# Row sums of a softmax taken over partitions by GpSimd instead of TensorE

## The chip, the cores and the metric

The kernel runs on one core of one Trainium2 chip. The metric is the device time of one execution in microseconds (us), as the median of several runs. Five engines with queues of their own share the core: TensorE (PE in the profile, with weight loads listed as PEld), VectorE (DVE), ScalarE (ACT), GpSimd (POOL) and SyncE (SP), which here issues nearly all DMAs.

## The reference

Attention through 49 agent tokens, then a two-layer network with a PReLU between the layers. Two batches of 12480 tokens, 128 channels, hidden width 2048, all in float32.

```
scale = 1 / sqrt(128)
a2k     = softmax(scale * agents @ k^T)        # 49 x 12480 per batch
agent_v = a2k @ v                              # 49 x 128
q2a     = softmax(scale * q @ agents^T)        # 12480 x 49
x       = q2a @ agent_v                        # 24960 x 128 over both batches
h       = x @ w_in                             # 128 -> 2048
g       = max(h, 0) + alpha * min(h, 0)
out     = g @ w_out                            # 2048 -> 128
```

softmax(s) is e / (sum of e + 1e-9) with e = exp(s - max). What this case is about is the sum over the 49 agents in q2a, one number per token.

## The kernel before, in words

**The main loop.** Tokens stand in columns. A group is 480 tokens, 52 groups in all, and two groups make a pair k (0 to 25). The hidden layer is cut into 8 steps per group, so that a pair has 16 steps and the loop 416. In step s TensorE first runs `g1(s+2)`: it multiplies the unnormalised exponentials of a group, split into a high part `qmh` and a low part `qml`, by `agent_v @ w_in` (tile `sab`), 6 matmuls of 64 rows by 480 columns, into the PSUM tile `h`, of which there are two. ACT takes the positive part of `h` rounded (`rh`, line 974), DVE what the rounding left (`rl`, line 975). Then `g2(s)` multiplies `rh` and `rl` by the second layer's weights, 12 matmuls (line 990), into the accumulator `acc` of the group. After a group's eighth step three more matmuls (line 1001) add the linear part of the PReLU; ACT and DVE take the result out (lines 1006 and 1007), DVE turns it (`o_take`, line 1012), multiplies it by the reciprocal of the softmax's sum (`o_scale`, line 1017), and SP stores it (`o_store`, line 1035). The reciprocal is thus needed only at the very end of a group.

A matmul of 64 rows uses half of the array's rows. Two of them, one on rows 0 to 63 and one on rows 64 to 127, run side by side; a pair of them is called a slot below.

**The chain that makes the exponentials of pair k.** Its functions, in order, with the step at which each is issued, counted from the first step of pair k, s0 = 16k: `q_transpose` (-18), `q_hi` and `q_lo` (-16), `q_logits` (-14, 8 matmuls, line 864), `q_take` and `q_swap` (-13: an ACT copy and two DMAs on SP that swap halves of the partitions into tile `qw`), `q_add` (-11, line 890), `q_max` (-10, GpSimd's maximum over all 128 partitions, line 894), `q_sub` (-7, line 899), `q_exp_hi` (-6, line 903), `q_exp` and `q_split` (-5, lines 908 and 912), `q_sum` (4), `q_spread` (5) and `q_rec` (10). The list `CHAIN` holds these steps; `CHAIN_1` and `CHAIN_0` hold those of pairs 1 and 0. Since the chain of pair k+1 begins 18 steps before its own first step, it stands between the steps of pair k. A function given to `pre` is issued ahead of the step's g1, one given to `at` between g1 and g2. Every engine works through its own instructions in this written order; semaphores hold an instruction until what it reads is written and the buffer it writes is free.

The logits stand twice, on partitions 0 to 63 and 64 to 127, and `padb` sends the rows beyond 49 to zero through the exponential.

**The part that is changed.** `q_sum` multiplies `qmh` and `qml` by a matrix of ones: 4 matmuls (line 923) into the spare half of PSUM, which gives each token's sum on all partitions. `q_spread` copies these sums to the tile `sums` in SBUF by ACT (line 933) and has SP issue one DMA (line 939) that lays the sums of 960 tokens over the partitions. `q_rec` turns that on DVE, adds 1e-9 and takes the reciprocal (lines 946 to 951).

Tiles: `qs` and `qm` have one buffer each. `qs` holds the turned queries, then the logits, then (in place) the exponentials; `qm` holds the swapped half `qw` and then the maximum.

**Other work in the loop.** Steps 8 to 95 also make the logits of the second batch's keys (lines 538, 552, 572 to 574, 591), steps 96 to 187 its exponentials and products with v (lines 608 to 660), and around step 200 the weights `sab` of the second batch are made. GpSimd has little to do: the maxima, one per pair, and in steps 96 to 187 small memsets (line 612).

Of the kernel before, what the change touches and what calls it, by code (L numbers as in the profile page):

```python
# [9 lines left out]
F32 = mybir.dt.float32  # L10
F32R = mybir.dt.float32r
U32 = mybir.dt.uint32
AF = mybir.ActivationFunctionType
ALU = mybir.AluOpType
# [8 lines left out]
KEYS = (((1, 0), 6, 7), ((5, 3), 9, 14), ((9, 12), 14, 16))  # L23
VALUES = ((((0, 3, 1, 1), (3, 1, 4, 4)), 6), (((3, 0, 7, 8), (2, 8, 5, 6)), 10))
FOLD = (189, 195, 198, 202, 205, 206)
CHAIN = (-18, -16, -16, -14, -13, -13, -11, -10, -7, -6, -5, -5, 4, 5, 10)
CHAIN_0 = (-19, -18, -18, -11, -9, -6, 1, 6, 10, 15, 17, 19)
CHAIN_1 = (-14, -13, -13, -11, -10, -10, -10, -10, -8, -7, -5, -5, 4, 5, 10)
EARLY = (1, 3, 6, 6)
OUT = (4, 5, 5)  # L30

# [24 lines left out]
def kernel(  # L56
# [11 lines left out]
    nc = tc.nc  # L68
# [4 lines left out]
    P = 128  # L73
    HALF = 64
    NF = DFF // P
    GT = 480
    TB = GT // 32
# [13 lines left out]
    SCALE = 1.0 / math.sqrt(C)  # L91
# [5 lines left out]
    p1 = ctx.enter_context(tc.tile_pool(name="p1", bufs=1))  # L97
# [12 lines left out]
    def pair_tile(name, i=None):  # L110

        i = (step[0] // NM + 1) % 2 if i is None else i
        return late[i].tile([P, 2, 512], F32, tag="x", name=name)
# [21 lines left out]
    padb = const.tile([P, 1], F32, name="padb")  # L135
# [655 lines left out]
    gq = {}  # L791
# [20 lines left out]
    def flat(t):  # L812
        return t.rearrange("p h n -> p (h n)")
# [90 lines left out]
        gq["mh", k] = m  # L904

    def q_exp(k):
        e = gq["e", k] = gq.pop(("s", k))
        nc.scalar.activation(out=e, in_=e, func=AF.Exp, bias=padb, scale=SCALE)

    def q_split(k):  # L910
        m = p2.tile([P, 2, GT], F32R, tag="qml", name=f"qml{k}")
        nc.vector.tensor_tensor(out=m, in0=gq["e", k], in1=gq["mh", k], op=ALU.subtract)  # L912
        mh = gq.pop(("mh", k))
        gq.pop(("e", k))
        gq["mhl", k] = (m, mh)
        for i in range(2):
            gq["M", 2 * k + i] = (mh[:, i, :], m[:, i, :])

    def q_sum(k):
        t = gq["sum_ps", k] = pair_tile(f"qsum{k}")  # L920
        for n, x in enumerate(gq.pop(("mhl", k))):
            for i, (r0, r1) in enumerate(TILES):
                nc.tensor.matmul(  # L923
                    t[:, i, 0:GT], lhsT=ones[r0:r1, :], rhs=x[r0:r1, i, :],
                    start=n == 0, stop=n == 1,
                )

    def q_spread(k):
        if "sums" not in gq:
            t = gq["sums"] = p1m.tile([P, 1024], F32, tag="qsum", name="qsum")  # L930
            nc.gpsimd.memset(t[:, 2 * GT :], 1.0)
        t = gq["sums"]
        nc.scalar.copy(
            out=t[:, 0 : 2 * GT].rearrange("p (h n) -> p h n", h=2),
            in_=gq.pop(("sum_ps", k))[:, :, 0:GT],
        )

        x = p1m.tile([P, 32], F32, tag="qx", name=f"qx{k}")
        nc.sync.dma_start(
            out=x, in_=t.rearrange("(c o) (i j) -> c o i j", c=4, j=32)[:, 0, :, :]  # L940
        )
        gq["sum", k] = x

    def q_rec(k):
        t = p1m.tile([P, 32], F32, tag="qst", name=f"qst{k}")
        nc.vector.transpose(out=t, in_=gq.pop(("sum", k)))
        r = p2.tile([P, 2, TB, 1], F32, tag="qr", name=f"qr{k}")
        nc.vector.tensor_scalar(
            out=r.rearrange("p h t o -> p (h t o)"), in0=t[:, 0 : 2 * TB], scalar1=1e-9, scalar2=None, op0=ALU.add
        )  # L950
        nc.vector.reciprocal(out=r, in_=r)
        for i in range(2):
            gq["r", 2 * k + i] = r[:, i]
# [68 lines left out]
    def o_store(g):  # L1022
# [14 lines left out]
    q_chain = [  # L1037
        q_transpose, q_hi, q_lo, q_logits, q_take, q_swap, q_add, q_max,
        q_sub, q_exp_hi, q_exp, q_split, q_sum, q_spread, q_rec,
    ]  # L1040

# [5 lines left out]
    with tc.manual_schedule():  # L1047
# [46 lines left out]
        for n in range(7):  # L1094
            load, ops = (load_win, narrow_win) if n < 4 else (load_wo, narrow_wo)
            s = SLABS[n]
# [11 lines left out]
        def more():  # L1108
            f = next(loads, None)
            if f is not None:  # L1110
                f[1](*f[2:])
            return f

        while n_in < N_IN:
            f = more()
            n_in += f[1] not in (q_load_rows, load_alpha, load_late)
        for s in range(max(plan) + 1):
            for f, a in plan.pop(s, ()):
                f(*a)
                if f.__name__ == "total" or f in (k_turn, k_mix):  # L1120
                    while True:
                        f = more()
# [5 lines left out]
        p1m = ctx.enter_context(tc.tile_pool(name="p1m", bufs=1))  # L1128
# [22 lines left out]
        for i2 in range(NGT // 2):  # L1151
            s0 = 2 * NM * i2
            if i2 == 0:
                at(10, q_sum, 0)
                pre(11, q_spread, 0)
                at(13, q_rec, 0)
                continue
            steps = CHAIN if i2 > 1 else CHAIN_1
            if i2 > 1:
                at(max(0, s0 - LEADS[2]), q_load, i2)  # L1160
            for f, i in zip(q_chain, steps):
                (pre if f in (q_take, q_swap, q_spread) else at)(s0 + i, f, i2)
# [93 lines left out]
```

## Time and profile before

| what | value |
|---|---|
| median of 3 runs | 987.12 us (987.0 to 988.08) |
| span of the profiled execution, first to last instruction | 985.9 us |
| the profiled execution's own time | not listed apart from its span |
| median of the runs less the span | 1.2 us |
| busy PE / DVE / ACT / POOL | 971.7 / 837.7 / 626.4 / 89.8 us |
| granted TensorE clock over the span | 0.998 of full speed |

Busy time of PE counts every moment at which a matmul runs, be it on one half of the rows or on both. The durations of single matmuls overlap, since they are pipelined: what one costs is read from the distance between the starts of two, not from its length. PE's list in the timeline is in order of the start; "x2" joins neighbours of one kind.

### The profile page before, as it was taken

How to read it: one execution, taken by the hardware profiler on the slowest of the kernel's cores; microseconds unless marked ns; L12 is line 12 of the kernel's file. 1: busy time of each engine (PE TensorE's matmuls, PEld its weight loads, DVE VectorE, ACT ScalarE, POOL GpSimd, SP SyncE). 2: the span in 40 equal slices, each digit the busy share in tenths (PEclk: the TensorE clock that was granted, in tenths of full speed). 3: DMA queues.
4: the chain of work that ended last, by engine and by line, in shares of the span. 5: the costliest groups of instructions: out<-in, count | busy, mean ns of one | idle time of the engine just before them, and what ended most of it. 6: DMA issues, size and time to landing. Idle time of an engine off the chain costs nothing.

```text
span 985.9 us, 21716 instructions
## 1 busy us (share of the span) xinstructions
PE 971.7 (99%) x9046; PEld 927.0 (94%) x9046; DVE 837.7 (85%) x1054; ACT 626.4 (64%) x779; POOL 89.8 (9%) x67
## 2 busy tenths in 40 slices
PE   8989999999999999999999999999999999999997
PEld 5658999999989999999987999999999999999997
DVE  7887988998899999999987788788878887888775
ACT  5765655655667767777765666666666666666563
POOL 0011011011011011001101101100110111011100
PEclk9999999999999999999999999999999999999999
DMA  9933354444234234234312222212221223121201
GB/s 342 361 51 63 65 84 87 81 70 88 42 75 80 62 73 95 45 70 95 65 31 44 42 51 41 53 37 46 52 53 31 42 55 56 35 41 33 42 11 31
DMA packets 281027, 69.51 MB, mean 71 GB/s; under 512 B 259119, under 2 KB 273953, under 8 KB 280929
## 3 DMA queue, kind: packets, MB, share of 16 engines
q1 hardware_dynamic: 279937, 68.00, 33.0%
q8 instruction: 71, 1.16, 0.5%
q10 hardware_dynamic: 992, 0.12, 0.1%
q14 instruction: 27, 0.22, 0.1%
HBM read 42.59 MB, written 12.78 MB: 56 GB/s over the span
## 4 chain that ended last, share of the span: by engine, by line
PE 94%; DVE 2%; DMA 2%; ACT 1%; issue 0%; SPq 0%; ACTq 0%
PE acc L990 55%; PE h L968 27%; PE lg L864 2%; PE kl L552 2%; PE acc L1001 2%; PE av L650 1%; PE qsum L923 1%; DMA kw<-in_k_dram 1%; DMA win<-in_moe_w_in_dram 1%; PE a_ps L726 0%; DVE red L414 0%; PE avw L471 0%; PE ktp L388 0%; PE lin_ps L784 0%; PE etp L451 0%
## 5 line engine op out<-in xcount | busy, mean ns | idle before, releaser
L975 DVE SCALAR_TENSOR_TENSOR rl<-h,rh 128x960 fp32r<-128x960 f32 x416 | 478.2, 1150 | 123.1 <-ACT rh L974 120.8
L974 ACT ACTIVATE rh<-h 128x960 fp32r<-128x960 f32 x416 | 404.3, 972 | 270.1 <-PE h L968 262.1
L968 PE MATMUL h<-qmh,sab 64*128 64x480 f32 x1664 | 401.3, 378 | 0.7 <-DVE rl L975 0.5
L990 PE MATMUL acc<-rh,wl 64*128 64x480 f32 x1664 | 400.3, 378 | 0.0
L990 PE MATMUL acc<-rh,wh 64*128 64x480 f32 x1664 | 398.0, 375 | 0.0
L990 PE MATMUL acc<-rl,wh 64*128 64x480 f32 x1664 | 313.2, 377 | 0.0
L968 PEld LDWEIGHTS h<-qmh,sab 64*128 64x128 f32 x1664 | 247.2, 185 | 7.5 <-DVE rl L975 2.5
L990 PEld LDWEIGHTS acc<-rh,wl 64*128 64x128 f32 x1664 | 246.9, 184 | 5.9 <-issue 2.3
L990 PEld LDWEIGHTS acc<-rh,wh 64*128 64x128 f32 x1664 | 247.6, 184 | 2.9
L990 PEld LDWEIGHTS acc<-rl,wh 64*128 64x128 f32 x1664 | 223.6, 184 | 3.2
L968 PE MATMUL h<-qml,sab 64*128 64x480 f32 x832 | 222.7, 377 | 0.0
L894 POOL PARTITION_ALL_REDUCE qm<-qs x26 | 85.6, 3293 | 768.0 <-DVE qs L890 731.3
L968 PEld LDWEIGHTS h<-qml,sab 64*128 64x128 f32 x832 | 128.0, 185 | 1.7 <-DVE qml L912 0.2
L1006 ACT COPY os<-acc 128x480 f32<-128x480 f32 x52 | 29.2, 561 | 33.8 <-PE acc L1001 33.6
L1007 DVE TENSOR_TENSOR os<-acc,os 128x480 f32<-128x480 f32 x52 | 33.9, 651 | 2.7 <-ACT os L1006 2.4
L1012 DVE STREAM_TRANSPOSE ot<-os 128x480 f32<-128x480 f32 x52 | 34.7, 668 | 0.0
L903 ACT ACTIVATE qmh<-qs,padb 128x960 fp32r<-128x960 f32 x26 | 28.5, 1097 | 9.2 <-DVE qs L899 9.2
L1017 DVE TENSOR_TENSOR ot<-ot,qr 128x480 f32<-128x480 f32 x52 | 33.6, 645 | 0.1
L899 DVE TENSOR_TENSOR qs<-qs,qm 128x960 f32<-128x960 f32 x26 | 29.8, 1148 | 0.5 <-POOL qm L894 0.5
L890 DVE TENSOR_TENSOR qs<-qs,qw 128x960 f32<-128x960 f32 x25 | 28.7, 1148 | 1.7 <-DMA qw<-qs 1.7
L912 DVE TENSOR_TENSOR qml<-qs,qmh 128x960 fp32r<-128x960 f32 x26 | 29.8, 1148 | 0.0
L827 DVE STREAM_TRANSPOSE qt<-qin 128x960 f32<-128x960 f32 x25 | 29.2, 1167 | 0.0
(172 smaller groups left out, 802.8 us busy)
## 6 DMA issues: line engine op xcount, KB each, us to landing
out_dram<-ot SPq DMA_DIRECT2D x206, 60.0 KB
qin<-in_q_dram SPq DMA_DIRECT2D x200, 60.0 KB
qw<-qs SPq DMA_DIRECT2D x50, 240.0 KB
kw<-in_k_dram SPq DMA_DIRECT2D x12, 512.0 KB
vw<-in_v_dram SPq DMA_DIRECT2D x12, 512.0 KB
kb<-in_k_dram SPq DMA_DIRECT2D x96, 64.0 KB
v<-in_v_dram SPq DMA_DIRECT2D x24, 256.0 KB
win<-in_moe_w_in_dram SPq DMA_DIRECT2D x4, 512.0 KB
```

The costliest lines, as they stand in the source:

```text
L827: nc.vector.transpose(out=flat(t), in_=gq.pop(("in", k)).rearrange("p h t i -> p (h t i)"))
L894: nc.gpsimd.partition_all_reduce(flat(t), flat(gq["s", k]), P, ReduceOp.max)
L899: nc.vector.tensor_tensor(out=t, in0=t, in1=gq.pop(("m", k)), op=ALU.subtract)
L912: nc.vector.tensor_tensor(out=m, in0=gq["e", k], in1=gq["mh", k], op=ALU.subtract)
L968: nc.tensor.matmul(h[:, u, 0:GT], lhsT=w[a][r0:r1, f0 : f0 + P], rhs=x[r0:r1, :], start=n == 0, stop=n == 2,)
L974: nc.scalar.activation(out=rh, in_=h[:, :, 0:GT], func=AF.Relu)
L975: nc.vector.scalar_tensor_tensor(out=rl, in0=h[:, :, 0:GT], scalar=0.0, in1=rh, op0=ALU.max, op1=ALU.subtract)
L990: nc.tensor.matmul(acc[:, i, 0:GT], lhsT=a[r0:r1, 2 * m + u, :], rhs=x[r0:r1, u, :], start=m == 0 and n == 0, stop=False,)
L1006: nc.scalar.copy(out=t, in_=acc[:, 0, 0:GT])
L1007: nc.vector.tensor_tensor(out=t, in0=acc[:, 1, 0:GT], in1=t, op=ALU.add)
L1012: nc.vector.transpose(out=t.rearrange("p t i -> p (t i)"), in_=oo.pop(g))
L1017: nc.vector.tensor_tensor(out=t, in0=t, in1=gq.pop(("r", g)).to_broadcast([P, TB, 32]), op=ALU.mult)
```

## The change

The sums of pair 0 stay as they are. For every other pair `q_sum` issues two GpSimd instructions instead of four matmuls: a copy of one column of `qml` to a small tile (`gate`), which has to wait until the split has written it, and a sum over all 128 partitions of the exponentials straight into the tile `sums`. The ACT copy of `q_spread` falls away for these pairs. As the logits stand twice, the sum comes out doubled, and `q_rec` halves it in the instruction that adds 1e-9. The exponentials go to a new tile in the buffer of `qm`, not in place into `qs`. `q_sum` moves from step 4 to step -5, `q_spread` from 5 to 1.

```diff
-CHAIN = (-18, -16, -16, -14, -13, -13, -11, -10, -7, -6, -5, -5, 4, 5, 10)
+CHAIN = (-18, -16, -16, -14, -13, -13, -11, -10, -7, -6, -5, -5, -5, 1, 10)
...
-CHAIN_1 = (-14, -13, -13, -11, -10, -10, -10, -10, -8, -7, -5, -5, 4, 5, 10)
+CHAIN_1 = (-14, -13, -13, -11, -10, -10, -10, -10, -8, -7, -5, -5, -5, 1, 10)
...
     def q_exp(k):
-        e = gq["e", k] = gq.pop(("s", k))
-        nc.scalar.activation(out=e, in_=e, func=AF.Exp, bias=padb, scale=SCALE)
+        s = e = gq.pop(("s", k))
+        if k:
+            e = p1.tile([P, 2, GT], F32, tag="qm", name=f"qe{k}")
+        gq["e", k] = e
+        nc.scalar.activation(out=e, in_=s, func=AF.Exp, bias=padb, scale=SCALE)
...
+    def sums():
+        if "sums" not in gq:
+            t = gq["sums"] = p1m.tile([P, 1024], F32, tag="qsum", name="qsum")
+            nc.gpsimd.memset(t[:, 2 * GT :], 1.0)
+        return gq["sums"]
+
     def q_sum(k):
+        e = gq.pop(("e", k))
+        if k:
+            m, _ = gq.pop(("mhl", k))
+            gate = p1m.tile([P, 1], F32, tag="gate", name=f"gate{k}")
+            nc.gpsimd.tensor_copy(gate, m[:, 1, GT - 1 : GT])
+            nc.gpsimd.partition_all_reduce(sums()[:, 0 : 2 * GT], flat(e), P, ReduceOp.add)
+            return
         t = gq["sum_ps", k] = pair_tile(f"qsum{k}")
...
     def q_spread(k):
...
-        nc.scalar.copy(
-            out=t[:, 0 : 2 * GT].rearrange("p (h n) -> p h n", h=2),
-            in_=gq.pop(("sum_ps", k))[:, :, 0:GT],
-        )
+        t = sums()
+        if k == 0:
+            nc.scalar.copy(
+                out=t[:, 0 : 2 * GT].rearrange("p (h n) -> p h n", h=2),
+                in_=gq.pop(("sum_ps", k))[:, :, 0:GT],
+            )
...
-            out=r.rearrange("p h t o -> p (h t o)"), in0=t[:, 0 : 2 * TB], scalar1=1e-9, scalar2=None, op0=ALU.add
+            out=r.rearrange("p h t o -> p (h t o)"), in0=t[:, 0 : 2 * TB], scalar1=0.5 if k else 1.0, scalar2=1e-9,
+            op0=ALU.mult, op1=ALU.add,
```

## Rows read from the trace of the kernel before

**Rows 1.** The page: busy time and share by engine; the chain's shares by engine
```profile
PE 971.7 (99%) x9046; PEld 927.0 (94%) x9046; DVE 837.7 (85%) x1054; ACT 626.4 (64%) x779; POOL 89.8 (9%) x67
...
PE 94%; DVE 2%; DMA 2%; ACT 1%; issue 0%; SPq 0%; ACTq 0%
```

**Rows 2.** Windows from one maximum to the next: stretch and length, busy time by engine
```profile
161.13:199.78 38.65, 38.65 (x407) 38.57 (x405) 34.64 (x43) 22.63 (x26) 3.31 (x1) 1.00 0.48 81
...
417.14:452.31 35.17, 35.17 (x342) 35.15 (x340) 33.31 (x45) 25.75 (x35) 3.54 (x5) 1.00 0.35 74
...
596.70:630.01 33.31, 33.31 (x310) 33.28 (x308) 27.48 (x31) 21.13 (x23) 3.31 (x1) 1.00 0.26 47
```

**Rows 3.** Waits of all engines, longest first: total us, times, longest
```profile
ACT rh L974 <- PE h L968: 262.1, 293, 2.0
DVE rl L975 <- ACT rh L974: 120.8, 193, 1.7
...
PEld h L968 <- DVE rl L975: 2.5, 5, 1.4
...
DVE qs L890 <- DMA qw<-qs: 1.7, 2, 1.2
```

**Rows 4.** Timeline of PE around one sum: start, duration, instruction
```profile
623.06 0.38 PE L968 MATMUL h<-qmh,sab 64*128 64x480 f32 x1
...
623.72 0.38 PE L923 MATMUL qsum<-qml,ones 64*128 64x480 f32 x1
...
624.24 0.38 PE L923 MATMUL qsum<-qmh,ones 64*128 64x480 f32 x1
...
625.47 0.38 PE L968 MATMUL h<-qmh,sab 64*128 64x480 f32 x1
...
627.42 0.38 PE L968 MATMUL h<-qmh,sab 64*128 64x480 f32 x1
```

**Rows 5.** All instructions of line 933: duration in ns, least, median, most
```profile
L933 ACT COPY qsum<-qsum x26: 942/954/958, 97.4 to 957.4; 128x960 f32<-128x960 f32 x26
```

**Rows 6.** Groups on GpSimd: count, busy us, mean ns, idle time before
```profile
L894 POOL PARTITION_ALL_REDUCE qm<-qs x26 | 85.6, 3293 | 768.0 <-DVE qs L890 731.3 <-DMA qin<-in_q_dram 36.6
...
L239 POOL CAST aq<-aq 64x64 fp32r<-64x64 f32 x4 | 1.0, 246 | 48.5 <-DVE aq L235 48.4
```

**Rows 7.** Timeline of DVE and PE after a split, late pair
```profile
607.70 1.15 DVE L912 TENSOR_TENSOR qml<-qs,qmh 128x960 fp32r<-128x960 f32 x1
...
611.47 0.64 DVE L1017 TENSOR_TENSOR ot<-ot,qr 128x480 f32<-128x480 f32 x1
...
612.14 1.16 DVE L975 SCALAR_TENSOR_TENSOR rl<-h,rh 128x960 fp32r<-128x960 f32 x1
...
614.34 0.38 PE L968 MATMUL h<-qmh,sab 64*128 64x480 f32 x1
```

**Rows 8.** A maximum on GpSimd, and DVE meanwhile; then line 632's least/median/most ns
```profile
382.26 3.04 POOL L894 PARTITION_ALL_REDUCE qm<-qs  x1 [27.50 <-DVE qs L890]
...
382.26 1.15 DVE L975 SCALAR_TENSOR_TENSOR rl<-h,rh 128x960 fp32r<-128x960 f32 x1
383.33 0.94 DVE L632 TENSOR_TENSOR e<-s,e 128x196 fp32r<-128x196 f32 x1
...
L632 DVE TENSOR_TENSOR e<-s,e x25: 247/352/935, 302.0 to 493.2; 128x196 fp32r<-128x196 f32 x24, 96x98 fp32r<-96x98 f32 x1
```

**Rows 9.** Timeline of SP: the swap's two DMAs, then the sums' DMA
```profile
621.33 1.12 SPq L883 DMA_DIRECT2D qw<-qs  x2
626.07 0.57 SPq L939 DMA_DIRECT2D qx<-qsum  x1
```

**Rows 10.** Timeline of DVE and PE later in the pair: the densest run
```profile
628.71 1.15 DVE L890 TENSOR_TENSOR qs<-qs,qw 128x960 f32<-128x960 f32 x1
...
630.35 2.37 DVE L975 SCALAR_TENSOR_TENSOR rl<-h,rh 128x960 fp32r<-128x960 f32 x2
...
631.77 0.47 PE L968 MATMUL h<-qmh,sab 64*128 64x480 f32 x2
```

More of the change, by code (lines that the diff above doesn't have):

```diff
@@ L913, in q_split @@
         mh = gq.pop(("mh", k))
-        gq.pop(("e", k))
         gq["mhl", k] = (m, mh)
@@ L928, in q_spread @@
     def q_spread(k):
[L929 to L932, printed above, removed]
-        nc.scalar.copy(
-            out=t[:, 0 : 2 * GT].rearrange("p (h n) -> p h n", h=2),
-            in_=gq.pop(("sum_ps", k))[:, :, 0:GT],
-        )
+        t = sums()
[4 more added lines that the diff above has]
+            )
         x = p1m.tile([P, 32], F32, tag="qx", name=f"qx{k}")
```

## The prediction, made before the change was run

> **What bounds the kernel now.** I read the page's busy times and chain first, then the windows by stage, then the waits, then the timeline around one sum. The page says that TensorE is busy nearly all the time and that the chain that ended last runs on it for 94% of the span [rows 1]. Busy time is a mean over stages with different limits, so the windows come next: cut from one maximum to the next, each holds one pair. In all three kinds of stage PE is busy for the whole window: 38.65 of 38.65 us while the second batch's keys are scored, 35.17 of 35.17 while its values are mixed in, 33.31 of 33.31 after that [rows 2]. The reader is to see there also what is left on the others: DVE is idle for 4.0, 1.86 and 5.8 us of a window, ACT for 9 us and more. The waits say the same from the other side: ACT waits for PE's `h` 293 times, 262 us in all, and DVE's `rl` for ACT; the wait of the main path in the other direction, PE's weight loads on `rl`, is 2.5 us in the whole run [rows 3]. So the bound is TensorE's stream of matmuls, and time goes down by what is taken out of that stream as long as the others keep up.
>
> **What the sums cost.** A late pair has 16 steps of 18 matmuls, 8 for the logits, 4 for the sums and 6 for the linear part: 306 matmuls, or 153 slots of two that run side by side, in 33.31 us, which is 0.218 us a slot. The sums' 4 matmuls are two slots: 0.435 us. The timeline gives it once more: the step that holds the sum takes from 623.06 to 625.47, 2.41 us, the next one from 625.47 to 627.42, 1.95 us; the difference is 0.46 [rows 4]. In that step the two halves of the array run 0.08 us out of phase, so that the difference of two starts can be off by some hundredths. I take 0.45 between the two. The change removes it from pairs 1 to 25, so 25 x 0.45 = 11.2 us, with 10.9 and 11.5 as the ends.
>
> **The other edits, each against its cover.**
> The ACT copy of the sums goes, 0.954 us for each of 25 pairs [rows 5], 24 us of ACT. ACT spends more than ten times that waiting for PE [rows 3], so I count it as nothing. It can't lengthen anything, and a gain would need an `rh` that is late because of the copy; with PE never waiting there is none to be had.
>
> GpSimd gets a small copy and a sum over partitions for each pair. The trace has no sum. The nearest row is the maximum of the same shape, 3.29 us on average [rows 6]; for the copy of one column the nearest is the cast of 64 columns, 0.25 us. For the sum's length I take the maximum's, 3.3 us, since it reads, folds and writes the same 960 columns; I keep 0.5 us below (nothing in the path would notice) and twice that, 6.6 us, above. GpSimd's two jobs lie far apart: the split of a late pair ends at 607.70 + 1.15 = 608.85 and the next maximum begins some 21 us later, after line 890's add [rows 7, 10]. The copy waits for the split, and queued behind it are only the sum, the memsets of line 612 for the following pair in the middle stage, and that maximum. With 0.2 us for the semaphore, 0.25 for the copy and 3.3 for the sum the queue is free at 612.6, about a step ahead of the next pair's first, where the first of those memsets has its place; the matmuls that read what it sets come six steps later. So the added wait costs nothing, and would cost nothing at 6.6 us either.
>
> The exponentials now sit in the buffer of `qm` until the sum is done. The next to write there are the two swap DMAs of the following pair, which SP issues at 621.33 [rows 9], 8.7 us after the sum's end. If they were late, the stores queued behind them on SP would be too; a sum of over 12 us would be needed for that. The exponential itself waits for nothing new, since line 899 has read the maximum before line 903 can start. `qs` comes free earlier, for which nobody waits.
>
> The sums' DMA (one per pair, 16 KB) moves on SP from behind the swap's two DMAs to ahead of them, and ahead of the loads of k, v and q that are issued in those four steps. It waits now for GpSimd instead of the ACT copy; at 612.6 it is ready, and the two DMAs that it passes wait for ACT until 621 anyway. Its reader, the reciprocal, keeps its place, 15 steps after the split. Nothing is gained or lost. The factor of one half rides in an instruction that exists already.
>
> **The one shared resource.** GpSimd and DVE can hold each other up, and the trace shows it. A maximum starts at 382.26; line 632, which reads two operands from SBUF, starts at 383.33 and takes 0.94 us where its median is 0.352 [rows 8]. With its own 0.352 us at the end it was let go at 383.92, 1.66 us after the maximum began and 1.4 us before the maximum's record ends. Line 975 reads one operand from PSUM and keeps its 1.15 us under the same maximum. So a sum holds up DVE instructions with two SBUF operands for its first 1.7 us. After the split come a line 975, a transpose, a line 975, and then line 1017, which has two SBUF operands, at 611.47 [rows 7]. That is 2.62 us after the split's end. The sum begins about 0.45 us after the split and lets go at 0.45 + 1.66 = 2.1 us: line 1017 is not touched. If it were, there is room: the `rl` behind it ends at 612.14 + 1.16 = 613.30, and PE takes the `h` buffer that this frees at 614.34, 1.04 us later [rows 7]. A hold that ends up to 2.62 + 1.04 = 3.66 us after the split is thus free. I count the contention as nothing, with nothing as its lower end, since GpSimd can only delay DVE.
>
> The Trainium skill is harder here ("SBUF — State Buffer", section "Who interferes with whom"): a DVE instruction with two SBUF inputs and a GpSimd instruction that reads SBUF exclude each other, and the later one blocks for the whole instruction. Our trace agrees that line 632 blocks and line 975 doesn't, but puts the release at 1.66 of 3.04 us, not at the end. By the page's rule the hold would last to 0.45 + 3.3 = 3.75 us after the split, a tenth of a us past the free 3.66, some 2 us over the run, and any longer sum would then cost in full.
>
> **The sum.** On the profiled execution: 985.9 - 11.2 = 974.7 us of span. Its own time isn't listed, so I add what the median of the runs has over the span, 1.2 us: 975.9 us, 1.1% below 987.1.
>
> **Rivals.**
> (a) DVE becomes the bound in the middle stage. There it is busy for 33.31 of 35.17 us [rows 2]; the saved 0.45 leaves it 1.4 us of slack, and its instructions come in runs. If none of the saving arrives in the six windows of that stage, 6 x 0.45 = 2.7 us are given back: 978.6. For it speaks the density; against it, that each run of DVE instructions follows an `rl` that itself waits for PE by way of ACT (193 times [rows 3]), so that the runs move forward together with PE.
> (b) The sum's slots filled a moment in which PE would have waited. After the sum DVE has its densest run, the add of line 890, line 1017 and two `rl` without a gap [rows 10]; if that run kept its place in time, PE would meet it early: the first of the two `rl` ends halfway, at 631.53, and PE takes that buffer at 631.77, 0.24 us later [rows 10]. PE would wait 0.45 - 0.24 = 0.2 us per pair, 5 us in all: 981. At the extreme all of it comes back and the time is 987.1. Against it: line 890 waits for its DMA in two cases only [rows 3], the run starts behind an `rl`, and this moves with PE.
> (c) The other sign: the sum takes longer than the maximum and keeps DVE out all that time. From 3.66 us after the split on, each us costs PE one us per pair, and at 3.66 + 0.45 = 4.1 us the gain is gone. A sum of 5 us (half as long again as the maximum) that holds to its end lets go at 5.45 us: (5.45 - 3.66) x 25 = 45 us lost, 975.9 + 45 = 1021. It needs both a longer sum and a hold that the maximum doesn't show; with the maximum's share of its length, 55%, even a sum of 5.8 us is free.
> (d) The change doesn't do what it says: the sum is so slow (12 us and more) that SP's queue stands behind it. The swap and stores would then be late, and the result is slower as in (c); I count it there.
>
> **How the numbers follow.** The forecast, with its own range of 975.0 to 977.5, gets 0.82. (a) gets 0.07, (b) 0.05, of which 0.02 for no change at all, (c) with (d) 0.06. A measurement of this kernel can tell about 0.2%, 2 us, from no change. Faster by more: 0.82 + 0.07 + 0.03 = 0.92; within: 0.02; slower: 0.06. The range is 974.5 (sums at 0.46 and an `rh` or two that come earlier without the ACT copy) to 979.5, which takes in (a) and leaves out (b) and (c).
>
> **What would show it.** PE still busy for the whole of each window; 100 fewer matmuls and only pair 0's four on line 923; a late window of 32.86 us instead of 33.31 and a key window of 38.2; the sum's record at 3.0 to 3.4 us, with its start right behind the split; line 1017 at its 0.65 us; SP's DMA of the sums right after the sum, before the swap's. The step "PE's slots are pure cost" is wrong if PE shows idle time behind `rl`; "the sum is like the maximum" is wrong if its record is past 4 us; "line 1017 is clear of it" is wrong if that line has a second length above 0.65 us. The prediction as a whole is wrong if the windows shrink by less than 0.35 us.

## The result: 0.8% slower, and the profile after

| | before | after |
|---|---|---|
| median of 4 runs each, same chip | 987.6 us (987.0 to 988.34) | 995.9 us (994.71 to 996.36) |
| span of the profiled execution | 985.9 us | 994.4 us |
| distance of two maxima, late pairs | 33.31 us | 33.78 us |

The ratio is 1.008, with a 95% interval of 1.0066 to 1.0095. The forecast was 975.9 us (974.5 to 979.5), so even the sign is wrong. The rival with the other sign, (c), came true in its first half: the sum is longer than the maximum, but it does not hold DVE to its end, and the price is smaller than the one given there.

The page after, first busy times, then the chain by engine and by line (line 989 is what line 975 was, 982 was 968, 1004 was 990, 1031 was 1017):

```profile
PE 976.7 (98%) x8946; PEld 837.2 (84%) x8946; DVE 872.1 (88%) x1054; ACT 606.8 (61%) x754; POOL 237.4 (24%) x117
...
PE 72%; DVE 19%; ACT 5%; issue 2%; SPq 1%; DMA 1%; POOL 0%; DVEq 0%; ACTq 0%
```

The 100 matmuls are gone, yet TensorE is busy for longer. DVE has the same 1054 instructions and 34 us more of busy time, and its part of the chain goes from 2% to 19% [rows 1]. An engine whose instructions last longer without being more is held up while it works. One line accounts for it, the multiplication by the reciprocal (`o_scale`), before and after (count, busy us, mean ns, idle time before):

```profile
L1017 DVE TENSOR_TENSOR ot<-ot,qr 128x480 f32<-128x480 f32 x52 | 33.6, 645 | 0.1
...
L1031 DVE TENSOR_TENSOR ot<-ot,qr 128x480 f32<-128x480 f32 x52 | 71.7, 1379 | 0.1
```

PE's busy time rose with fewer matmuls, so it now holds time in which they made no headway, and its share says little; the windows say more (columns as in [rows 2]):

```profile
162.66:201.29 38.63, 38.63 (x400) 34.32 (x400) 35.62 (x43) 21.93 (x26) 9.21 (x3) 1.00 0.48 81
...
419.16:454.59 35.43, 35.41 (x336) 32.56 (x335) 34.68 (x45) 24.97 (x34) 9.38 (x8) 1.00 0.36 74
...
599.88:633.66 33.78, 33.51 (x306) 28.28 (x304) 28.98 (x31) 20.38 (x22) 9.21 (x4) 1.00 0.25 45
```

A late pair has four matmuls fewer and takes 0.47 us more; in the last row PE is idle for 0.27 us, which it never was [rows 2], and DVE has 1.5 us more for the same 31 instructions. The waits show the place at which the path now turns (columns as in [rows 3]):

```profile
ACT rh L988 <- PE h L982: 290.2, 314, 2.0
POOL gate L932 <- DVE qml L915: 249.1, 25, 13.1
DVE rl L989 <- ACT rh L988: 93.6, 159, 1.8
...
PEld h L982 <- DVE rl L989: 22.0, 47, 1.4
```

PE's loads now wait for `rl` 47 times, 22.0 us, where it was 5 times and 2.5 us [rows 3]. What delays `rl` is seen in GpSimd's groups (columns as in [rows 6]) and in the timeline after a split, which answers to [rows 7]:

```profile
L933 POOL PARTITION_ALL_REDUCE qsum<-qe x25 | 143.7, 5747 | 0.2 <-issue 0.2
L894 POOL PARTITION_ALL_REDUCE qm<-qs x26 | 85.9, 3305 | 416.3 <-DVE qs L890 379.7 <-DMA qin<-in_q_dram 36.5
L932 POOL COPY gate<-qml 128x1 f32<-128x1 f32 x25 | 4.7, 189 | 249.1 <-DVE qml L915 249.1
```

```profile
611.13 1.15 DVE L915 TENSOR_TENSOR qml<-qe,qmh 128x960 fp32r<-128x960 f32 x1
...
612.34 0.18 POOL L932 COPY gate<-qml 128x1 f32<-128x1 f32 x1 [9.14 <-DVE qml L915]
612.49 5.75 POOL L933 PARTITION_ALL_REDUCE qsum<-qe  x1
613.26 0.67 DVE L1026 STREAM_TRANSPOSE ot<-os 128x480 f32<-128x480 f32 x1
613.85 1.12 DVE L989 SCALAR_TENSOR_TENSOR rl<-h,rh 128x960 fp32r<-128x960 f32 x1
614.89 2.35 DVE L1031 TENSOR_TENSOR ot<-ot,qr 128x480 f32<-128x480 f32 x1
617.17 1.15 DVE L989 SCALAR_TENSOR_TENSOR rl<-h,rh 128x960 fp32r<-128x960 f32 x1
618.37 0.49 PE L982 MATMUL h<-qmh,sab 64*128 64x480 f32 x2 [0.27 <-DVE rl L989]
```

The sum over 960 columns takes 5.75 us, 1.7 times the maximum of the same shape. Line 1031, which reads two operands from SBUF, should take 0.65 us; it takes 2.35. With its own 0.65 at the end it was let go at 616.59, which is 4.10 us after the sum's start and 1.65 before its record ends. The `rl` behind it ends at 618.32, and PE, which wants the `h` that this frees, starts at 618.37, after a wait. The `rl` and the transpose that run under the same sum keep their 1.12 to 1.15 and 0.67 us. In 24 of the 25 pairs line 1031 meets the sum and is let go 4.10 or 4.11 us after its start. Two SBUF operands are not the whole condition, though. The sum of pair 1 also meets the `q_rec` of pair 0, whose line 961 reads one SBUF tile and takes 0.18 us otherwise:

```profile
102.03 5.75 POOL L933 PARTITION_ALL_REDUCE qsum<-qe  x1
...
104.66 1.65 DVE L961 TENSOR_SCALAR qr<-qst 128x30 f32<-128x30 f32 x1
```

With its own 0.18 us at the end it was let go at 106.13, again 4.10 us after the start. What sets it apart from the transpose isn't shown.

### The profile page after: what moved, and what is told of

The parts are those of the page before. It is cut to its first block, busy times and chain, and to the rows that moved or that the text cites. A ratio compares the mean times of both kernels' runs of the same rounds, so it can differ in the third digit from the quotient of the medians.

```text
span 994.4 us, 21546 instructions
## 1 busy us (share of the span) xinstructions
PE 976.7 (98%) x8946; PEld 837.2 (84%) x8946; DVE 872.1 (88%) x1054; ACT 606.8 (61%) x754; POOL 237.4 (24%) x117
## 3 DMA queue, kind: packets, MB, share of 16 engines
q8 instruction: 70, 1.15, 0.5%
## 4 chain that ended last, share of the span: by engine, by line
PE 72%; DVE 19%; ACT 5%; issue 2%; SPq 1%; DMA 1%; POOL 0%; DVEq 0%; ACTq 0%
PE acc L1004 41%; PE h L982 22%; DVE rl L989 8%; DVE ot L1031 3%; ACT rh L988 3%; PE lg L864 2%; PE kl L552 2%; DVE qs L899 1%; DVE qml L915 1%; PE av L650 1%; PE acc L1015 1%; DVE ot L1026 1%; ACT qmh L903 1%; DVE red L414 1%; SPq L801 1%
## 5 line engine op out<-in xcount | busy, mean ns | idle before, releaser
L982 PE MATMUL h<-qmh,sab 64*128 64x480 f32 x1664 | 376.1, 382 | 5.8 <-DVE rl L989 5.5
L1004 PE MATMUL acc<-rh,wl 64*128 64x480 f32 x1664 | 375.0, 380 | 0.0
L1004 PE MATMUL acc<-rh,wh 64*128 64x480 f32 x1664 | 372.1, 377 | 0.0
L982 PEld LDWEIGHTS h<-qmh,sab 64*128 64x128 f32 x1664 | 224.1, 184 | 41.0 <-DVE rl L989 22.0
L1004 PEld LDWEIGHTS acc<-rh,wl 64*128 64x128 f32 x1664 | 223.1, 184 | 23.4 <-issue 2.3
L1004 PEld LDWEIGHTS acc<-rh,wh 64*128 64x128 f32 x1664 | 224.3, 184 | 20.1
L1004 PEld LDWEIGHTS acc<-rl,wh 64*128 64x128 f32 x1664 | 194.1, 184 | 21.0
L982 PE MATMUL h<-qml,sab 64*128 64x480 f32 x832 | 202.2, 377 | 0.0
L933 POOL PARTITION_ALL_REDUCE qsum<-qe x25 | 143.7, 5747 | 0.2 <-issue 0.2
L1031 DVE TENSOR_TENSOR ot<-ot,qr 128x480 f32<-128x480 f32 x52 | 71.7, 1379 | 0.1
```

The lines of the kernel that those rows point to most:

```text
L933: nc.gpsimd.partition_all_reduce(sums()[:, 0 : 2 * GT], flat(e), P, ReduceOp.add)
L982: nc.tensor.matmul(h[:, u, 0:GT], lhsT=w[a][r0:r1, f0 : f0 + P], rhs=x[r0:r1, :], start=n == 0, stop=n == 2,)
L1004: nc.tensor.matmul(acc[:, i, 0:GT], lhsT=a[r0:r1, 2 * m + u, :], rhs=x[r0:r1, u, :], start=m == 0 and n == 0, stop=False,)
L1031: nc.vector.tensor_tensor(out=t, in0=t, in1=gq.pop(("r", g)).to_broadcast([P, TB, 32]), op=ALU.mult)
```

## The experiments

The theory: the sum's length lets it hold line 1031, and through the `rl` queued behind it PE. The rivals: the 100 matmuls were worth nothing, or the rest of the change (gate, place of the exponentials, order on the queues) costs the time. Each kernel ran beside the kernel before, whose medians were 987.78 to 987.97 us.

**x1: everything but the sum.**

```diff
-            nc.gpsimd.partition_all_reduce(sums()[:, 0 : 2 * GT], flat(e), P, ReduceOp.add)
+            sums()
```

> The sum over partitions of pairs 1 to 25 is left out (their tokens are divided by pair 0's sums); everything else of the change stays: four matmuls and the ACT copy fewer, the small copy that waits for the split, the other tile, the moved DMA. Theory 1 (the sum on GpSimd holds DVE's line 1031, and through it TensorE): the whole forecast saving appears, about 976 us, late window 32.87 us, line 1031 at 0.65 us throughout. Rival (the loss comes from another part of the change: the moved DMA, the tile, the two halves of the array out of phase): it stays near 996 us with windows near 33.8.

979.56 us, ratio 0.9916 [0.9902, 0.9931]. A late window of x1 (columns as before):

```profile
592.63:625.64 33.01, 33.01 (x306) 32.99 (x304) 27.50 (x31) 20.29 (x22) 3.49 (x3) 1.00 0.26 46
```

PE is busy throughout again, and the window is 33.78 - 33.01 = 0.77 us shorter. Against its own kernel before, the changed kernel stands at +8.3 us and x1 at -8.2: the sum alone costs 16.5 us. But 0.45 a pair should have given -11.2, so 3 us are missing that have nothing to do with the sum. The rival about the rest of the change is wrong on the sign and right on a remainder.

**x2: the same instruction in the same place, as a maximum.**

```diff
-            nc.gpsimd.partition_all_reduce(sums()[:, 0 : 2 * GT], flat(e), P, ReduceOp.add)
+            nc.gpsimd.partition_all_reduce(sums()[:, 0 : 2 * GT], flat(e), P, ReduceOp.max)
```

> The sum over partitions becomes a maximum over partitions in the same place (so the tokens are divided by half the largest exponential). Theory 1a (it is the length of the sum: 5.75 us where the maximum takes 3.3, with DVE let go about 1.4 us before the end of either): the instruction takes 3.0 to 3.3 us, line 1031 is clear of it, about 976 us. Rival 1b (any GpSimd instruction that reads SBUF in this place blocks line 1031 to its end): line 1031 is held to 3.3 us after the start, some 0.9 us longer than 0.65, of which the free 1.04 us swallows nearly all: 976 to 978 us, but with line 1031 near 1.5 us. Rival 2 (not GpSimd): 996 us.

979.14 us, 0.9913 [0.9898, 0.9928], late window 33.01. In its timeline:

```profile
604.64 3.04 POOL L933 PARTITION_ALL_REDUCE qsum<-qe  x1
...
607.05 0.64 DVE L1031 TENSOR_TENSOR ot<-ot,qr 128x480 f32<-128x480 f32 x1
```

With the maximum's length line 1031 begins 2.41 us after the start and isn't held, though the record goes on to 3.04. It is not the trouble, then, that GpSimd reads and writes there: line 1031 has to come while the hold lasts, and the hold ends before the record does. What the prediction assumed gives what it expected, but for the 3 us.

**x3: the sum stays, line 1031 of even groups goes two steps later.**

```diff
-OUT = (4, 5, 5)
+OUT = (4, 7, 5)
```

> The changed kernel with line 1031 (o_scale) of the even groups issued two steps later, at step 15 instead of 13, after the sum has let DVE go; the store moves with it. The sum stays as long as it is. Theory 1 (what costs is that line 1031 meets the sum): line 1031 at 0.65 us, about 976 us, late window about 32.9. Rival (GpSimd's reading slows DVE whatever it runs, or TensorE is held by something else): 985 to 996 us.

981.25 us, 0.9935 [0.9919, 0.9952].

```profile
605.08 5.75 POOL L933 PARTITION_ALL_REDUCE qsum<-qe  x1
...
611.43 0.64 DVE L1031 TENSOR_TENSOR ot<-ot,qr 128x480 f32<-128x480 f32 x1
```

The sum is as long as before; the late window is 33.01, as without any sum. That one instruction is the whole loss in these windows. The second and third windows together are 1.2 us longer than in x1, where the new order seems to suit less.

**x4: the sum held back until behind line 1031.** The sum goes from step -5 to -2, and the gate copies a column of that line's output.

```diff
-CHAIN = (-18, -16, -16, -14, -13, -13, -11, -10, -7, -6, -5, -5, -5, 1, 10)
+CHAIN = (-18, -16, -16, -14, -13, -13, -11, -10, -7, -6, -5, -5, -2, 1, 10)
...
-            nc.gpsimd.tensor_copy(gate, m[:, 1, GT - 1 : GT])
+            nc.gpsimd.tensor_copy(gate, oo["n", 2 * k - 2][:, TB - 1, 31:32])
```

> The changed kernel with the sum held back until line 1031 of the even group is done (the small copy reads its output instead of the split's; issued at step 14 instead of 11). Theory 1: the sum then runs beside lines 989, 827, 989, 1021, 989, of which none has two SBUF inputs, and lets go some 4.1 us after its start, about when line 845 begins: line 1031 at 0.65 us, line 845 at 1.13 or a few tenths more, about 976 us, at most 978. Rival: 996 us, since the sum still runs once per pair beside DVE.

984.7 us, 0.9968 [0.9956, 0.9979]: the late windows are 33.01 as expected, the time is not. One window, in which the second batch's weights are made, takes 41.64 us:

```profile
502.64 5.75 POOL L933 PARTITION_ALL_REDUCE qsum<-qe  x1
...
502.72 4.44 DVE L688 TENSOR_TENSOR x<-x,rs 98x256 f32<-98x256 f32 x1
```

Line 688 takes 0.42 us in x1; here the sum holds it for 4.0, PE stands still for 2.71 us, until 508.28, for an `rl`. Then the granted clock falls (columns as in [rows 2], the clock behind the busy times):

```profile
508.00:510.50 2.50, 2.22 (x12) 1.85 (x14) 2.50 (x4) 0.81 (x1) 0.38 (x1) 0.61 0.04 7
```

The hold has only found another instruction.

**x6: the kernel before, with the sum added and read by nobody.** All 100 matmuls stay; gate and sum go behind the split, the sum into an unused tile.

```diff
+            nc.gpsimd.tensor_copy(gate, m[:, 1, GT - 1 : GT])
+            t = p1m.tile([P, 2 * GT], F32, tag="spare", name=f"spare{k}")
+            nc.gpsimd.partition_all_reduce(t, flat(e), P, ReduceOp.add)
```

> The kernel before with its matmul sums kept, and beside them, for pairs 1 to 25, the small copy and the sum on GpSimd into a tile that nobody reads (the exponentials in the buffer of qm, as in the change). Theory 1: the sum costs the same here as in the changed kernel, which lost 995.9 - 979.6 = 16.3 us to it, 0.77 us per late window: about 1004 us (1001 to 1007), late window 34.0 to 34.1, the line of o_scale (1017 in the kernel before) held to about 2.3 us. Rival (the sum only hurts once TensorE has been made faster, since DVE then has less slack): 988 to 995 us.

1006.63 us, 1.019 [1.0173, 1.0207], the late windows at 34.18 to 34.23.

```profile
617.91 5.75 POOL L922 PARTITION_ALL_REDUCE spare<-qe  x1
...
620.31 2.35 DVE L1025 TENSOR_TENSOR ot<-ot,qr 128x480 f32<-128x480 f32 x1
```

The same 5.75 and the same 2.35 us stand beside the full stream of matmuls, and +18.8 us is the 16.5 of x1 and the 2.7 that y2 below finds, within half a microsecond. What the sum costs doesn't depend on what it replaces.

**x9: two sums of 480 columns.**

```diff
-            nc.gpsimd.partition_all_reduce(sums()[:, 0 : 2 * GT], flat(e), P, ReduceOp.add)
+            for h in range(2):
+                nc.gpsimd.partition_all_reduce(sums()[:, h * GT : (h + 1) * GT], e[:, h, :], P, ReduceOp.add)
```

> The changed kernel with the sum in two instructions of 480 columns each, one after the other, nothing else moved. If the length goes with the columns and DVE is let go a fixed 1.4 to 1.6 us before an instruction's end, each takes about 3 us and lets go after 1.5 us or a little more: line 1031, which asks some 2.4 us after the first one's start, finds the gap, takes 0.65 to 1 us, and the time is near that without any sum, 979 to 982 us. If instead the two hold DVE as long as the one did, 4.1 us without a gap, line 1031 stays above 2 us and the time near 996.

986.31 us, 0.9983 [0.9974, 0.9992]. The two together take longer (x2 joins neighbours), and line 1032, the old 1031, lies between the holds in a late window but not while keys are scored:

```profile
179.45 6.08 POOL L934 PARTITION_ALL_REDUCE qsum<-qe  x2
...
182.45 2.65 DVE L1032 TENSOR_TENSOR ot<-ot,qr 128x480 f32<-128x480 f32 x1
...
611.48 6.08 POOL L934 PARTITION_ALL_REDUCE qsum<-qe  x2
...
613.88 0.64 DVE L1032 TENSOR_TENSOR ot<-ot,qr 128x480 f32<-128x480 f32 x1
```

At 2.40 us after the start it passes free; at 3.00 it meets the second sum and waits. Late windows are 33.01, key windows 39.5 to 39.7 where x1 has 38.3. So the run, 986.31 us, lies between the two expectations. The place in the sum that an instruction meets decides, not how much sum there is.

**x5: no gate, so that the sum may start with the split.**

```diff
-            gate = p1m.tile([P, 1], F32, tag="gate", name=f"gate{k}")
-            nc.gpsimd.tensor_copy(gate, m[:, 1, GT - 1 : GT])
```

> The changed kernel without the small copy: the sum starts as soon as the exponentials are there, at about the time at which the split (line 915, two SBUF inputs) starts. Theory 1: whichever comes second is held. If the sum gets in first, the split is held for some 4 us, and with it the rl behind it, against a slack of half a us there: TensorE loses about 3 us a pair and the time is 1050 to 1080 us. If the split gets in first, the sum starts when it ends and everything is as in the changed kernel, 994 to 997 us. Rival (what counts is line 1031 alone): with the sum 1.2 us earlier line 1031 is held 1.2 us less, about 982 us.

1122.43 us, 1.1362 [1.1327, 1.1397]:

```profile
609.77 5.75 POOL L931 PARTITION_ALL_REDUCE qsum<-qe  x1 [11.87 <-ACT qe L911]
609.81 5.23 DVE L915 TENSOR_TENSOR qml<-qe,qmh 128x960 fp32r<-128x960 f32 x1
...
616.16 0.48 PE L980 MATMUL h<-qmh,sab 64*128 64x480 f32 x2 [2.73 <-DVE rl L987]
```

Both wait for the same exponential; the sum is first by 0.04 us and the split loses 4.08 us, and so it goes in 24 of the 25 pairs. PE then waits 2.73 us for its `rl` here and 3.3 to 4.0 us in the others of these, and the mean granted clock over the run is 0.937 against 0.998, which the expectation had not counted. The gate, whose 249 us of waiting cost nothing, is worth 126 us.

**x7: x3 with the halves of the array swapped in the three matmuls of the linear part.** It asked after the missing 3 us: a step without other work takes 1.957 us (a mean over the late pairs) from one g1 to the next in the kernel before and 1.967 in the changed one and in the other experiments so far but x5.

```diff
-            if g % 2:
+            if g % 2 == 0:
```

> The kernel with o_scale two steps later (981 us), and the three matmuls of the linear part dealt out the other way round: even groups now use the rows 0 to 63 twice, odd groups the rows 64 to 127. Question: plain steps take 1.967 us in every kernel without the matmul sums and 1.957 in the kernel before, which is where 0.14 us per pair of the forecast saving went. If it is decided by which half of the array runs ahead, and by how much, the steps change here, to 1.95 to 1.96 at best: 977 to 978 us. If it is not, 981 us as before with steps of 1.967.

980.94 us, 0.993 [0.9916, 0.9945]; the step stays at 1.967. How these three matmuls are dealt out to the halves makes no difference; that the half that leads changed with it is not shown.

**y1 and y2: the place of the tiles.** The gate tile of 4 bytes a partition gets 32 from the allocator, and the tiles behind it move by these 32. Of those TensorE reads `rh` and `rl`: they start 32 bytes past a multiple of 64 in the kernel before, and at a multiple of 64 with the gate. x5 has no gate tile, `rh` and `rl` where the kernel before has them, and steps of 1.957. So y1 is x3 with a gate tile of 64 bytes, which puts them 32 past a multiple again, and y2 is the kernel before with one unused tile of 4, set once.

```diff
-            gate = p1m.tile([P, 1], F32, tag="gate", name=f"gate{k}")
+            gate = p1m.tile([P, 16], F32, tag="gate", name=f"gate{k}")[:, 0:1]
...
+            pad = p1m.tile([P, 1], F32, tag="gate", name="gate1")
+            nc.gpsimd.memset(pad, 0.0)
```

> The kernel with o_scale two steps later (981.25 us), its tile gate allocated 64 bytes wide per partition instead of 4, of which the copy still writes 4. The allocator gives a small tile 32 bytes, so that in every kernel with the tile gate so far the tiles behind it (the outputs ot, and rh and rl, which TensorE reads) lie 32 bytes further on than in the kernel before: rh and rl at multiples of 64 bytes, where the kernel before, and the one without the small copy and its tile, have them 32 bytes off one. Those two have plain steps of 1.957 us, all others 1.967. Theory 2 (the place of the tiles): with gate 64 bytes wide rh and rl are 32 bytes off again, plain steps take 1.957 us, late windows 32.85, and the time falls by about 4 us to 977 us. Rival (what is missing of the forecast has another cause): 981 us and 1.967.

> The kernel before with one small tile more, set once and read by nobody, allocated where the change has its gate; its ot, rh and rl move by 32 bytes, nothing else changes. Theory 2: plain steps go from 1.957 to 1.967 us, some 416 x 0.010 = 4 us: 991 to 992 us. Rival: 987.8 us.

y1: 978.41 us, 0.9905 [0.9891, 0.9918], against x3's 0.9935. y2: 990.7 us, 1.0027 [1.0017, 1.0038]. A late window of y1, then one of y2:

```profile
592.59:625.45 32.86, 32.86 (x306) 32.86 (x304) 27.35 (x31) 20.30 (x22) 9.21 (x4) 1.00 0.26 46
```

```profile
597.30:630.74 33.44, 33.44 (x310) 33.39 (x308) 27.50 (x31) 21.12 (x23) 3.31 (x1) 1.00 0.26 46
```

The wider tile takes 0.15 us off the window with nothing else changed; the unused one adds 0.13 to the kernel before, and 2.7 us to its run. The step goes to 1.957 in y1 and to 1.967 in y2. The runs change by 3 us or a little less where the expectations had 4. That the tiles' place does it is shown both ways; which of the moved tiles it is, and why TensorE cares, is not.

**y3: y1 with line 1031 one step later in place of two.**

```diff
-OUT = (4, 5, 5)
+OUT = (4, 6, 5)
```

> As the kernel with the 64-byte gate, but o_scale only one step later than in the change (step 14). In the kernel with step 15 the sum lets DVE go about 4.1 us after its start, at 609.2, and step 14 would put line 1031 behind the rl that ends at 609.4. Theory 1: it just clears the sum, 976 to 977.5 us, line 1031 at 0.65 us in late pairs; perhaps a little less than with step 15, since the first pair is disturbed less. Rival: it is still held in the stages where DVE runs ahead, 980 us and more.

977.2 us, 0.9892 [0.9879, 0.9906], faster than both kernels. Line 1031 (all 52 in ns, least, median, most), and a sum with that line:

```profile
L1031 DVE TENSOR_TENSOR ot<-ot,qr x52: 609/647/657, 107.5 to 970.5; 128x480 f32<-128x480 f32 x52
```

```profile
603.67 5.75 POOL L933 PARTITION_ALL_REDUCE qsum<-qe  x1
...
608.93 0.61 DVE L1031 TENSOR_TENSOR ot<-ot,qr 128x480 f32<-128x480 f32 x1
```

It comes 5.26 us after the sum's start, free of the hold, while the record lasts to 5.75, and none of the 52 is long any more; in the changed kernel the longest took 2609 ns.

## Why the prediction was wrong, step by step

**The step that failed** is "For the sum's length I take the maximum's, 3.3 us, since it reads, folds and writes the same 960 columns". It is 5.75 us. The upper end kept beside it, 6.6 us, held it; the forecast, its range and the 6% for (c) did not use that end. Two of the signs that the prediction itself named for being wrong came: a record past 4 us and a second length of the line above 0.65 us. Why a sum takes 1.7 times as long as a maximum isn't shown.

**Why that end looked harmless** is a second failed step: "with the maximum's share of its length, 55%, even a sum of 5.8 us is free". One hold of 1.66 us in 3.04 [rows 8] was read as a share. The trace of before had five more holds of line 632, under longer maxima; one of them:

```profile
346.75 3.31 POOL L894 PARTITION_ALL_REDUCE qm<-qs  x1 [27.21 <-DVE qs L890]
...
348.14 0.88 DVE L632 TENSOR_TENSOR e<-s,e 128x196 fp32r<-128x196 f32 x1
```

With its own 0.35 us at the end it was let go at 348.67: 1.92 us after the start and 1.39 before the end, where the other maximum has 1.66 and 1.38. So between two maxima of different length the rest is the same to 0.01 us, while the share goes from 55 to 58%. The sum of 960 columns holds for 4.1 us of 5.75, 71%, with a rest of 1.65. Read as "all but the last 1.4 us", the rows give a hold of 4.35 us for a sum of 5.75, and the step's own rule would have shown the loss. The rest is no law either: the second sum of x9 lets line 1032 go 1.08 us before the end of its record.

**That rule held.** A hold was to be free up to 3.66 us after the split's end [rows 7] and cost one for one beyond. The sum begins 0.21 us after the split (0.45 was taken) and lets go at 616.59 - 612.28 = 4.31, so 0.65 us a pair; measured 0.77 in a late window and 16.5 us over 25 pairs, 0.66 each. That the mean agrees so well is in part luck: between x1 and the changed kernel a window of the middle stage grows by 0.56 us, and key windows by 0.15 to 0.47, since line 1031 meets the sum later there. That the instruction would be line 1017, and that the damage would go through the `rl` behind it to PE's `h`, is as written. By the Trainium skill's rule ("SBUF — State Buffer", section "SBUF: two separate sides"), a lock for the whole instruction, the hold would have lasted to 0.21 + 5.75 = 5.96 us after the split and cost 2.3 us a pair; the trace is milder, 0.77, but with the sum's own length the rule has the sign that the prediction missed.

**A term was missing**: where the new tile pushes the others. 2.7 us (y2), which no row of before could show.

**What was right.** The sums' slots: 0.45 us a pair was said, and y1 and y3 have the late window at the 32.86 us that was forecast; y3 saves 10.8 us in the run for the 11.2. The ACT copy, the gate's wait, the exponentials in `qm`'s buffer and the sums' DMA ahead of the swap's cost nothing that shows: with them all x1 keeps PE busy for its whole window, and y1 has the window that was forecast. Rival (a) did not come: the middle window is 34.87 us in x1 and 34.74 in y3, from 35.17, so DVE let all of the saving through. Nor did (b), or (d). The sum ends at 612.49 + 5.75 = 618.24, and SP issues its DMA behind the stores that it has begun, 6 us ahead of the swap's:

```profile
617.27 1.95 SPq L1049 DMA_DIRECT2D out_dram<-ot  x4
619.32 0.58 SPq L952 DMA_DIRECT2D qx<-qsum  x1
625.36 1.13 SPq L883 DMA_DIRECT2D qw<-qs  x2
```

**The sum as it should have been**, for a late pair: 33.31 - 0.45 (matmuls, y1) + 0.15 (tiles, x3 against y1) + 0.77 (hold, x1) = 33.78. These terms are differences of neighbouring runs, so they add up to the measured window by construction; what tests them are runs that stand outside the row, y2 (0.13 for the tiles) and x6, which has the sum and the tiles beside all matmuls (34.20 less 33.31 is 0.89, where 0.15 + 0.77 is 0.92). For the run: -10.8 (y3) + 2.7 (y2) + 16.5 (x1) = +8.4 us for the +8.3 measured.

## What to carry to other kernels

A sibling's time is not an operation's time: when a new GpSimd instruction is priced from the nearest row, work the sum out at the far end of the bound too, and give the other sign the chance that this end has. Before GpSimd gets a long job, mark where DVE's instructions with two SBUF operands (and, by line 961, some with one) stand in the queue that feeds the bound engine; the cure may be one number that moves one of them (x3: from 8.3 us above the kernel before to 6.5 below it). After adding a tile, however small, compare a step that the change doesn't touch; if it has moved, pad the tile.

## What the hardware showed that was not expected

- A sum over 128 partitions of 960 fp32 columns takes 5.75 us on GpSimd where the maximum takes 3.04 to 3.31; a sum of 480 takes 3.09.
- The sum of 960 columns shuts out a DVE instruction with two SBUF operands until 1.65 us before its record ends, and one with a single SBUF operand too (line 961). Ready by the same exponential, the sum is first by 0.04 us (x5), and the split loses over 4 us.
- With the tiles behind the gate 32 bytes further on, `rh` and `rl` among them, a step of 18 matmuls goes from 1.957 to 1.967 us, 0.5%; with 64 bytes it is back at 1.957 (y1).
- Behind PE's one wait of 2.71 us in x4 the granted clock is 0.61 from 508.0 to 510.5 and 0.50, the lower of its two levels (1.2 of 2.4 GHz), from 508.6 to 511.9. In x5, where PE waits 2.7 to 4.0 us in nearly every pair, its mean over the run is 0.937.
